# Attention and a two-layer network on one core: weight sums placed by a table, one x sum moved into the block, loads and filling laid anew, more idle matmuls

## The chip, the cores and the metric

The kernel runs on one core of a Trainium2 chip. The time is the device time of one execution in microseconds (us). Before the change it is 371.84 us, the median of three runs (371.81 to 371.89).

## What is computed

The reference, cut to what matters (q, k, v are 8 batches x 12 heads x 448 positions x 64; w_in is 768 x 2048, w_out 2048 x 768):

```python
scores = q @ k.transpose(0, 1, 3, 2) / sqrt(64) - log(448)
attn   = 1 / (1 + exp(-scores))                  # a sigmoid, no softmax
x      = (attn @ v).transpose(0, 2, 1, 3).reshape(3584, 768)
h      = x @ w_in
g      = h * (1 / (1 + exp(-beta * h)))
out    = g @ w_out
```

The kernel works in fp16 with sums in fp32.

## The kernel before

**Attention.** A *quad* g is four heads of one batch; there are 24, three to a batch. Its q and k are loaded, cast to fp16 by the DMA (`load_one`, L121), and turned by VectorE (`transpose`, L193). A *visit* (`visit`, L271) computes the scores of one quad for one tile of 128 keys, as eight matmuls that run in four row groups of the array (sixteen where the last 64 keys of two quads are taken together), and ScalarE turns them into weights with one sigmoid over four PSUM banks (`weigh_two`, L251; in the first part of the program `weigh`, L240, over two). When all keys of a quad are there, `attend` (L318) multiplies the weights with v, sixteen matmuls, and VectorE casts the result into xT (L349). v's last 64 rows are copied to the other half of the partitions first (`double_v_last`, L160).

**The dense layers** fill TensorE between visits. `early` (L729) holds the first layer of batch 0 (`dense1`, L368, L377) with ScalarE's sigmoid (L394) and VectorE's product, the gate (L395), and the second layer of tiles 0 and 1 (`plain`, L408); `second_batch` (L764) the first layer of batch 1. Some partial results of batch 0 are put aside into SBUF by VectorE (L389) and brought back into a PSUM bank by ScalarE (`bring`, L363) before they are finished. From there on the second layer goes in pairs of tiles by a scheme with seven products in place of eight (`strassen`, L633, L644), and the first layer of batches 2 and 3, 4 and 5, 6 and 7 in three *blocks* of the same scheme (`blocks`, L540, L522). The schemes need sums: of parts of w_in (S1 to S4, `in_sum`, L474), of w_out (T1, T3, T4, T6, T7, `weight_sum`, L455), of x (`x_sums`, L490) and of g (L631). VectorE makes all of them; each weight sum is cut into two parts, 18 instructions in all.

**What sets the order.** The order is written by hand (`tc.manual_schedule`); each engine runs its instructions in the order in which the program issues them. `LOADS` and `LATER` order the loads on GpSimd's queue. `BEGIN` (L858) lists the first part of the program: casts, transposes, scores, idle matmuls (`idle_units`, L840, matmuls on zeros whose result is not used), attends, dense units. Then comes a loop over 74 visits (L972). `UNITS[n]` says how many dense matmuls follow visit n, `LATE[n]` after how many of them a waiting attend is placed (99: not in this visit). `some_sum` (L908) issues one weight sum in each visit until all are made. The first x sums are issued in visits from the list `soon`, what is left of it in `first_layer` (L961) before the block starts.

**Banks.** PSUM has eight banks. In the first part of the program six belong to the scores, from `two` on four, in the blocks none; `bank` (L84) gives out the least recently used of the rest.

## Time and profile before

| What | Value |
|---|---|
| median of three runs | 371.84 us |
| profiled execution, its own time | 371.74 us |
| its span | 370.0 us |
| busy: TensorE / VectorE / ScalarE / GpSimd | 361.8 / 262.7 / 259.6 / 85.1 us |
| granted TensorE clock | 1.00 |
| software DMA queue | 22.47 MB, 40.1% of the 16 engines' span |

The span is that of the profiled execution from its first to its last instruction; 1.74 us lie around it. A row of the order of time has its start, its duration, the engine and line, the operation and in brackets the idle time before it with what ended it. TensorE's matmuls are pipelined and their ends are modelled, so starts are safer than ends. In a row of the busy time by stretch stand, after the stretch, its length and then busy time (with the count) of TensorE's matmuls, its weight loads, VectorE, ScalarE and GpSimd, then the granted clock, the DMA engines' busy share and GB/s. The chain of waits is followed back from the last instruction. Visits are numbered from 0, as the loop numbers them; visit 0 starts at 36.30 us, visit 6 at 52.69 us.

### The profile page before, as it was taken

To read this page: it belongs to the slowest core of one execution; us is meant where nothing else is said; L and a number is where in the kernel's file an instruction comes from. 1 tells how busy PE (TensorE), PEld (TensorE's weight loads), DVE (VectorE), ACT (ScalarE), POOL (GpSimd) and SP (SyncE) were. 2 spreads that over 40 slices of the span, in tenths; PEclk is the share of its full clock that TensorE was granted. 3 is DMA by queue.
4 is the path that set the end of the run, shared out by engine and by line. 5 is a ranking of instruction groups with operands and counts; after the bars stand their busy time and mean duration, and the time that the engine had idled before them with its cause. 6 is when DMAs were issued, how large, how long until landed. Compare 5 with 4: busy or idle time off the path is not lost.

```text
span 370.0 us, 6995 instructions
## 1 busy us (share of the span) xinstructions
PE 361.8 (98%) x2750; PEld 176.3 (48%) x2750; DVE 262.7 (71%) x486; ACT 259.6 (70%) x308; POOL 85.1 (23%) x125
## 2 busy tenths in 40 slices
PE   8899999999999999999999999999999999999996
PEld 5334444344444455544444455554444455556664
DVE  2636878875687876785766986779766678688664
ACT  5977967898867578877777758887777758870000
POOL 7633543311130022341131002337100002220000
PEclk9999999999999999999999999999999999999999
DMA  9999999856093110099359211004913030002332
GB/s 170 205 209 204 202 205 202 193 71 97 6 168 90 43 44 1 0 139 159 63 92 200 56 44 43 1 2 65 204 44 85 2 85 2 1 2 63 87 103 90
DMA packets 32416, 34.62 MB, mean 94 GB/s; under 512 B 9328, under 2 KB 28416, under 8 KB 32384
## 3 DMA queue, kind: packets, MB, share of 16 engines
q0 software_dynamic: 26400, 22.47, 40.1%
q1 hardware_dynamic: 5984, 11.71, 11.7%
q8 instruction: 21, 0.34, 0.4%
q14 instruction: 11, 0.09, 0.1%
HBM read 45.62 MB, written 11.01 MB: 153 GB/s over the span
## 4 chain that ended last, share of the span: by engine, by line
PE 92%; ACT 5%; DMA 1%; DVE 1%; issue 0%; SPq 0%; ACTq 0%
PE ps L644 33%; PE ps L522 26%; PE ps L229 12%; PE ps L377 10%; PE ps L335 10%; ACT attns L242 2%; ACT attns L257 2%; PE ps L408 2%; DMA gt<-in_q_dram 1%; DVE osb L663 0%; DVE xT L349 0%; DVE ps L582 0%; ACT raw L826 0%; DVE qT L200 0%; PE ps L842 0%
## 5 line engine op out<-in xcount | busy, mean ns | idle before, releaser
L257 ACT ACTIVATE attns<-ps,nlogs 128x1792 f16<-128x1792 f32 x74 | 129.9, 1755 | 42.4 <-PE ps L229 42.3
L644 PEld LDWEIGHTS <-sum 128*128 128x128 f16 x536 | 49.0, 98 | 41.7 <-issue 13.0
L536 POOL TENSOR_TENSOR gt<-attns,sg 128x448 f16<-128x448 f32 x21 | 23.9, 1139 | 146.2 <-ACT sg L533 146.2
L644 PE MATMUL ps<-w_T,sum 128*128 128x384 f16 (+2 forms) x328 | 57.5, 319 | 0.0
L229 PE MATMUL ps<-qT,kT 32*128 32x448 f16 (+3 forms) x800 | 51.9, 353 | 3.6 <-ACT attns L242 1.9
L533 ACT ACTIVATE sg<-ps,beta_sb 128x448 f32<-128x448 f32 x72 | 45.2, 632 | 8.4 <-PE ps L522 5.9
L522 PE MATMUL ps<-xT,w_S 128*128 128x448 f16 x216 | 49.2, 352 | 0.1
L522 PE MATMUL ps<-xT,w_in 128*128 128x448 f16 x216 | 49.2, 352 | 0.0
L536 DVE TENSOR_TENSOR gt<-ps,sg 128x448 f16<-128x448 f32 x72 | 44.3, 619 | 3.5 <-ACT sg L533 3.3
L663 DVE TENSOR_TENSOR osb<-ps,osb 128x384 f32<-128x384 f32 (+2 forms) x67 | 36.1, 540 | 13.1 <-PE ps L644 11.8
L349 DVE CAST xT<-ps 128x448 f16<-128x448 f32 (+1 forms) x50 | 27.9, 600 | 24.1 <-PE ps L335 24.0
L522 PEld LDWEIGHTS <-w_in 128*128 128x128 f16 x288 | 28.1, 98 | 26.4 <-issue 0.4
L335 PE MATMUL ps<-attns,v 128*64 128x448 f16 (+3 forms) x400 | 40.4, 353 | 0.0
L377 PE MATMUL ps<-xT,w_in 128*128 128x448 f16 x192 | 39.7, 353 | 0.0
L631 DVE TENSOR_TENSOR sum<-gt 128x1024 f16<-128x1024 f16 x57 | 38.4, 690 | 0.2
L644 PE MATMUL ps<-w_out,sum 128*128 128x384 f16 x208 | 37.9, 327 | 0.0
L644 PE MATMUL ps<-w_out,gt 128*128 128x384 f16 (+2 forms) x200 | 36.8, 321 | 0.0
L582 DVE TENSOR_TENSOR ps<-ps,attns 128x448 f32<-128x448 f32 x24 | 15.2, 632 | 23.4 <-PE ps L522 22.0
L522 PEld LDWEIGHTS <-w_S 128*128 128x128 f16 x216 | 21.1, 98 | 19.6 <-issue 0.3
L125 POOL DMA_DIRECT2D raw<-in_q_dram x24 | 13.4, 559 | 69.1 <-DVE kT L212 56.2
L229 PEld LDWEIGHTS <-kT 32*128 32x128 f16 (+1 forms) x800 | 13.5, 96 | 32.6 <-issue 30.2
L395 DVE TENSOR_TENSOR gt<-ps,sg 128x448 f16<-128x448 f32 x32 | 18.9, 619 | 14.1 <-ACT sg L394 13.9
(54 smaller groups left out, 346.6 us busy)
## 6 DMA issues: line engine op xcount, KB each, us to landing
out_dram<-osb SPq DMA_DIRECT2D x98, 96.0 KB, 1.9
raw<-in_q_dram POOLq DMA_DIRECT2D x23, 224.0 KB, 6.2
raw<-in_k_dram POOLq DMA_DIRECT2D x23, 224.0 KB, 6.7
v<-in_v_dram POOLq DMA_DIRECT2D x16, 192.0 KB, 8.1
w_out<-in_moe_w_out_dram POOLq DMA_DIRECT2D x4, 768.0 KB, 15.8
v<-in_v_dram POOLq DMA_DIRECT2D x16, 144.0 KB, 8.1
w_in<-in_moe_w_in_dram POOLq DMA_DIRECT2D x3, 512.0 KB, 11.1
w_in<-in_moe_w_in_dram POOLq DMA_DIRECT2D x3, 256.0 KB, 8.0
```

Source lines behind the costliest of these rows:

```text
L229: nc.tensor.matmul(sco[base : base + nk, hh, u0 : u0 + n], kT[g][lo : lo + BLK, jt * P : jt * P + nk, e], qT[g][lo : lo + BLK, c0 : c0 + n ...
L257: nc.scalar.activation(out=attns[:, slot : slot + 2].rearrange("p n h s -> p (n h) s"), in_=sco, func=AF.Sigmoid, bias=nlogs[:, 0:1], scal ...
L335: nc.tensor.matmul(av[hh * D : (hh + 1) * D, 0:n], vs[b][base : base + nk, 2 * (s % NPAIR) + hh, jt], at[base : base + nk, hh, 0:n], start ...
L349: nc.vector.tensor_copy(out=xTs[b][:, s % NPAIR, c0 : c0 + n], in_=av)
L377: nc.tensor.matmul(m1, w_in16[:, hc, dc * P : (dc + 1) * P], xTs[b][:, hc], start=fresh, stop=(hc == hi - 1), skip_group_check=lo > 0,)
L395: nc.vector.tensor_tensor(out=gt[:, dc, off : off + S], in0=m1, in1=sg, op=ALU.mult)
L522: nc.tensor.matmul(out, w[:, c, i * P : (i + 1) * P], m[:, c], start=(start and c == 0), stop=(c == KH - 1), skip_group_check=not start,)
L533: nc.scalar.activation(out=sg, in_=h, func=AF.Sigmoid, bias=0.0, scale=beta_sb[:, dc : dc + 1])
L536: return lambda: engine.tensor_tensor(out=gt[:, dc, b % 2 * S : b % 2 * S + S], in0=h, in1=sg, op=ALU.mult)
L631: nc.vector.tensor_tensor(out=sums[t, i], in0=x, in1=y, op=op)
L644: nc.tensor.matmul(m2, (x if op is None else sums[t, i])[:, dc], w[:, dc, lo:hi], start=first, stop=(dc == ND - 1), skip_group_check=i >= 4,)
L663: nc.vector.tensor_tensor(out=out, in0=in0, in1=in1, op=op)
```

## The change

- *Weight sums.* A table now says in which visit each of the 18 parts is issued, on VectorE as before. Before, one part was issued in each visit from visit 0 on, where its condition allowed it.
- *Asides.* For two of the five (3 and 4) VectorE brings the partial result back into PSUM, not ScalarE.
- *Last x sum.* The last of the x sums before a block is issued inside it, behind the first sum of D.
- *Loads.* Load 3 comes before load 4, and load 5 goes ahead of w_out's first quarter and of the second v.
- *Filling.* `UNITS` and `LATE` have new numbers, and `BEGIN` orders its last dense work and the transposes of quad 3 differently.
- *Idle matmuls.* 14 more of 256 columns, and 5 of 448 columns (`busy`), which write a bank of their own from `bank`.

The diff, cut to its core (of the tables a few lines):

```diff
+    BY_VECTOR = (3, 4)
...
-        nc.scalar.copy(out=m2s[0, dc].rearrange("p (a c) -> p a c", a=2), in_=aside(dc))
+        copy = nc.vector.tensor_copy if dc in BY_VECTOR else nc.scalar.copy
+        copy(out=m2s[0, dc].rearrange("p (a c) -> p a c", a=2), in_=aside(dc))
...
-    def blocks(b: int, other, scores: int):
+    def blocks(b: int, other, last_sum, scores: int):
...
                 nc.vector.tensor_tensor(out=D, in0=B, in1=p5, op=ALU.add)
+                while last_sum:
+                    last_sum.pop()()
...
-            ("qk", 4), ("qk", 3), ("w_in", 12, 16), ("w_out", 0, 0), ("values", 1), ("w_out", 1, 0), ("qk", 5),
+            ("qk", 3), ("qk", 4), ("w_in", 12, 16), ("qk", 5), ("w_out", 0, 0), ("values", 1), ("w_out", 1, 0),
...
+        def busy_units(n: int):
+            to = bank()
+            for _ in range(n):
+                nc.tensor.matmul(to, still[:, 0:P], still[:, 0:S], start=True, stop=True)
...
-            ("idle", 20), ("scores", 0, 0, 1), ("idle", 4), ("scores", 0, 0, 0), ("q", 0, 1), ("idle", 2), ("k", 1),
-            ("q", 1, 0), ("idle", 4), ("scores", 0, 1, 0), ("idle", 6), ("scores", 0, 1, 1), ("v", 0), ("q", 1, 1),
+            ("idle", 20), ("scores", 0, 0, 1), ("idle", 8), ("scores", 0, 0, 0), ("q", 0, 1), ("idle", 6), ("k", 1),
+            ("q", 1, 0), ("idle", 4), ("scores", 0, 1, 0), ("idle", 10), ("scores", 0, 1, 1), ("busy", 3), ("v", 0),
...
-            ("values", 1, 1), ("two",), ("visit", 2, 2), ("dense", 4), ("values", 2, 3), ("values", 2, 0),
+            ("loads",), ("values", 1, 1), ("busy", 2), ("two",), ("visit", 2, 2), ("values", 2, 3), ("dense", 4),
...
+        sums_todo = [
+            ("S3", 0, 0), ("S2", 0, 0), ("S3", 1, 1), ("S2", 1, 4), ("S4", 1, 5), ("T7", 1, 7), ("S4", 0, 9),
+            ("T1", 1, 11), ("T6", 0, 13), ("T7", 0, 13), ("T1", 0, 14), ("T3", 0, 15), ("T6", 1, 16), ("T3", 1, 16),
+            ("T4", 0, 17), ("T4", 1, 19), ("S1", 0, 29), ("S1", 1, 33),
+        ]
...
-            12, 11, 14, 9, 2, 13, 9, 10, 11, 2, 10, 0, 9, 11, 12, 11, 2, 10, 1, 10, 13, 10, 13, 2, 13, 13, 2, 11, 11,
+            11, 11, 11, 7, 2, 11, 12, 11, 12, 2, 11, 2, 11, 11, 11, 2, 11, 10, 2, 11, 10, 11, 13, 3, 12, 12, 1, 12,
...
-            while soon:
+            while len(soon) > 1:
                 soon.pop(0)()
...
-            blocks(b, fill_units, 2 if b < B - 2 else 0)
+            blocks(b, fill_units, soon, 2 if b < B - 2 else 0)
...
-            some_sum()
+            some_sums(n)
```

In the new table of sums the third number is the visit. The lines of the changed program stand a few lines lower than those of the old one (L395 is L397 there, L482 L484, L501 L503, L582 L584).

VectorE's order at visits 0 to 4, around the first weight sums (L482) and the copy of the second v's last rows (L163), before:

```order
29 L482 TENSOR_TENSOR w_S_99<-w_in_90 128x3x512
30 L395 TENSOR_TENSOR gt<-ps,sg 128x448 x2
31 L200 STREAM_TRANSPOSE qT<-raw 128x448
32 L482 TENSOR_TENSOR w_S_99<-w_in_90 128x3x512
33 L395 TENSOR_TENSOR gt<-ps,sg 128x448 x2
34 L212 STREAM_TRANSPOSE kT<-raw 128x2x4x32
35 L212 STREAM_TRANSPOSE kT<-raw 128x2x3x32
36 L482 TENSOR_TENSOR w_S_98<-w_in_90,w_S_99 128x3x512
37 L395 TENSOR_TENSOR gt<-ps,sg 128x448 x3
38 L482 TENSOR_TENSOR w_S_98<-w_in_90,w_S_99 128x3x512
39 L163 COPY v_403<-v_403 64x12x64
40 L200 STREAM_TRANSPOSE qT<-raw 128x448
```

and in the changed program (L484 the sums, L368 the two asides that VectorE brings back, L397 the gates):

```order
30 L368 COPY ps<-gt 128x448
31 L397 TENSOR_TENSOR gt<-ps,sg 128x448
32 L484 TENSOR_TENSOR w_S_99<-w_in_90 128x3x512
33 L484 TENSOR_TENSOR w_S_98<-w_in_90,w_S_99 128x3x512
34 L368 COPY ps<-gt 128x448
35 L397 TENSOR_TENSOR gt<-ps,sg 128x448 x2
36 L200 STREAM_TRANSPOSE qT<-raw 128x448
37 L484 TENSOR_TENSOR w_S_99<-w_in_90 128x3x512
38 L397 TENSOR_TENSOR gt<-ps,sg 128x448 x2
39 L212 STREAM_TRANSPOSE kT<-raw 128x2x4x32
40 L212 STREAM_TRANSPOSE kT<-raw 128x2x3x32
41 L397 TENSOR_TENSOR gt<-ps,sg 128x448 x2
42 L163 COPY v_423<-v_423 64x12x64
```

The copy of v has three sums ahead of it in place of four, the two asides stand among them, and the second part of S2 is behind it.

VectorE's order where the third block begins, before (L501 the x sums, L582 the first sum of D):

```order
310 L349 COPY xT<-ps 128x448 x2
311 L501 TENSOR_TENSOR xT<-xT 128x448
312 L501 TENSOR_TENSOR xT<-xT 128x896 x2
313 L501 TENSOR_TENSOR attns<-xT 128x1344
314 L582 TENSOR_TENSOR ps<-ps,attns 128x448
315 L536 TENSOR_TENSOR gt<-ps,sg 128x448
316 L663 TENSOR_TENSOR osb<-ps,osb 128x384
```

and in the changed program (L503 and L584):

```order
314 L349 COPY xT<-ps 128x448 x2
315 L503 TENSOR_TENSOR xT<-xT 128x448
316 L503 TENSOR_TENSOR xT<-xT 128x896 x2
317 L584 TENSOR_TENSOR ps<-ps,attns 128x448
318 L503 TENSOR_TENSOR attns<-xT 128x1344
319 L538 TENSOR_TENSOR gt<-ps,sg 128x448
320 L667 TENSOR_TENSOR osb<-ps,osb 128x384
```

The last x sum, of 1344 columns into attns, has changed places with the first sum of D.

TensorE's order after the last scores of quad 0, before:

```order
199 L229 LDWEIGHTS kT
200 L229 MATMUL ps<-qT,kT 64x224
201 L229 LDWEIGHTS kT
202 L229 MATMUL ps<-qT,kT 128x448
203 L229 LDWEIGHTS kT
```

and in the changed program (L851 the wide idle matmuls):

```order
223 L229 LDWEIGHTS kT
224 L229 MATMUL ps<-qT,kT 64x224
225 L851 LDWEIGHTS gt
226 L851 MATMUL ps<-gt 128x448
227 L851 LDWEIGHTS gt
228 L851 MATMUL ps<-gt 128x448
229 L851 LDWEIGHTS gt
230 L851 MATMUL ps<-gt 128x448
231 L229 LDWEIGHTS kT
232 L229 MATMUL ps<-qT,kT 128x448
```

Three matmuls on zeros with their weight loads stand ahead of the next visit's scores.

More of the change, by code (lines that the diff above doesn't have):

```diff
@@ L880 @@
                 idle_units(a[0])
+            elif what == "busy":
+                busy_units(a[0])
             elif what == "v":
@@ L901, with some_sums @@
         fill += list(pairs(3, 5))
-        sums_todo = [(in_sum, n, p, 0) for n in ("S3", "S2", "S4") for p in range(2)]
-        sums_todo += [(weight_sum, n, p, 0) for n in ("T7", "T6", "T1") for p in range(2)]
-        sums_todo += [(weight_sum, n, p, L1B) for n in ("T4", "T3") for p in range(2)]
-        sums_todo += [(in_sum, n, p, L1E + 4 * ND) for n in ("S1",) for p in range(2)]
-        def some_sum(n: int = 1):
-            for _ in range(n):
-                if sums_todo and at_fill[0] >= sums_todo[0][3] and (sums_todo[0][0] is in_sum or (g, jt) > (QPB + 1, 1)):
-                    f, name, part, _ = sums_todo.pop(0)
-                    f(name, part)
+        sums_todo = [
[3 rows of a table added]
+        ]
+        ready_at = {"T4": L1B, "T3": L1B, "S1": L1E}
+        behind = {"S2": ("S3",), "S4": ("S2",), "S1": ("S3",), "T4": ("T7", "T1"), "T3": ("T6",)}
+        made = set()
+        def some_sums(n: int):
+            while sums_todo and sums_todo[0][2] <= n:
+                name, part, _ = sums_todo.pop(0)
+                assert at_fill[0] >= ready_at.get(name, 0)
+                assert all((x, part) in made for x in behind.get(name, ()))
+                made.add((name, part))
+                (in_sum if name in us else weight_sum)(name, part)
         visits = [(QPB, jt, ()) for jt in range(JF + 1)]
```

10 lines of the change are left out of this document (5 added, 5 removed), and 13 rows, old and new, of tables (LATE, UNITS).

## The prediction

> **What bounds the kernel now.** I read the page's chain of waits first, then the busy time by stretch, then TensorE's order of time where TensorE has gaps.
>
> ```profile
> PE 92%; ACT 5%; DMA 1%; DVE 1%; issue 0%; SPq 0%; ACTq 0%
> ```
>
> ```profile
> 5.50:24.20 18.70, 16.10 (x200) 7.18 (x201) 9.00 (x25) 17.62 (x20) 9.54 (x15) 1.00 1.23 201
> 52.70:70.00 17.30, 16.32 (x148) 7.26 (x148) 12.58 (x21) 12.27 (x8) 3.64 (x7) 1.00 1.16 214
> 70.00:94.50 24.50, 24.44 (x209) 9.95 (x209) 15.29 (x28) 22.94 (x25) 4.87 (x9) 1.00 0.60 86
> ```
>
> The chain is TensorE's for 92%: the time is what TensorE streams plus its pauses, and an edit pays only where it removes a pause or a switch. Two stretches have pauses. From 5.5 to 24.2 us ScalarE is busy 17.62 of 18.70 us and sets the pace. From 52.7 to 70.0 TensorE lacks 1 us though no engine is full (ScalarE 12.27, VectorE 12.58 of 17.3). Its order of time there shows why; the starts are what I use, since ends are modelled:
>
> ```profile
> 52.69 0.57 PE L229 MATMUL ps<-qT,kT 32*128 32x448 f16 x8
> 53.19 1.64 PE L408 MATMUL ps<-w_out,gt 128*128 128x384 f16 x9
> 55.18 0.60 PE L229 MATMUL ps<-qT,kT 32*64 32x448 f16 x16 [0.35 <-ACT attns L257]
> ...
> 60.59 1.64 PE L335 MATMUL ps<-attns,v 64*64 64x448 f16 x16
> 62.16 0.50 PE L408 MATMUL ps<-w_out,gt 128*128 128x384 f16 x2
> 62.59 0.57 PE L229 MATMUL ps<-qT,kT 32*128 32x448 f16 x8
> ...
> 67.58 0.58 PE L229 MATMUL ps<-qT,kT 32*128 32x448 f16 x8 [0.34 <-ACT attns L257]
> 68.08 1.88 PE L377 MATMUL ps<-xT,w_in 128*128 128x448 f16 x9
> 70.06 0.57 PE L229 MATMUL ps<-qT,kT 32*128 32x448 f16 x8
> ```
>
> ```profile
> 53.37 1.75 ACT L257 ACTIVATE attns<-ps,nlogs 128x1792 f16<-128x1792 f32 x1 [1.03 <-PE ps L229]
> ```
>
> A visit (L229) fills all four score banks, ScalarE needs 1.75 us to empty them, and only then may the next visit start: 52.69 (visit), 53.37 (ScalarE starts), 55.12 (done), 55.18 (next visit). This **loop** takes 2.43 to 2.49 us. A visit itself takes 0.50 (52.69 to 53.19), or 0.53 with sixteen matmuls, so the filling between two visits must last some 1.95 us or TensorE waits. What filling lasts comes from the chain's unstalled pieces:
>
> ```profile
> 58.23 1.90 PE ps L408 x11
> ...
> 73.36 2.38 PE ps L377 x12
> ...
> 76.25 2.19 PE ps L377 x11
> ```
>
> An L377 matmul is 2.38 - 2.19 = 0.19, and every change of kind costs 0.11 (11 x 0.19 is 2.08, not 2.19); an L408 (an L644 has its shape) is then (1.90 - 0.11) / 11 = 0.163. Eleven L408 with a visit make 2.41: at the limit; twelve are free.
>
> **The change, part by part.**
>
> *The table of filling (UNITS, LATE).* Visits 6 to 11 of the old table run from 52.69 to 67.58: 14.89. Their filling is 9 L408 (1.58), 10 (1.74), 11 (1.90), attend and 2 (1.57 + 0.43), 7 and 3 (7 x 0.163 + 3 x 0.19 + 0.11 = 1.82), attend alone (1.57): 10.61, with five visits of 0.51 and one of 0.53 13.69. So 1.20 of waiting. Visit 12 has 9 L377: 68.08 to 70.06 is 1.98 against 2.19 - 2 x 0.19 = 1.81: 0.17. The new table gives visits 6 to 12 the fillings 12, 11, 12, 2 with an attend, 11 (ten and one), an attend with 2, and 11: each 1.95 or more but visit 7. These 1.37 go. Two visits at 107 have the same trouble:
>
> ```profile
> 107.43 0.58 PE L229 MATMUL ps<-qT,kT 32*128 32x448 f16 x8
> ...
> 109.92 0.60 PE L229 MATMUL ps<-qT,kT 32*64 32x448 f16 x16
> ...
> 112.45 0.58 PE L229 MATMUL ps<-qT,kT 32*128 32x448 f16 x8
> ```
>
> 2.49 and 2.53, with eleven L644 each (2.41 and 2.43): 0.18, and the new table has twelve there. In all **-1.55**. New visits of eleven L408 stand at 5 and 7: 0.02 to 0.06 each, **+0.07**. Past 200 us both tables have nine visits of about 2.41: nothing. Counted in the order of TensorE from visit 0 on, both streams hold the same matmuls, and the new one has one switch more: **+0.10**.
>
> *The sums on VectorE.* Eighteen sums before, eighteen after, 0.94 each; only their places move. One old place hurts:
>
> ```profile
> 48.23 1.80 PE ps L335 x16
> ```
>
> ```profile
> 47.69 0.65 DVE L163 COPY v<-v 64x768 f16<-64x768 f16 x1
> ```
>
> This attend takes 1.80, not 1.57: it waits for the copy of v's last rows, which stands behind a sum (S2) and ends at 48.34. The new order has three sums ahead of the copy instead of four, with S2's second part behind it: by the durations of its queue I count it done by 46.5, and the attend needs it at 47.1. **-0.23**. Later eight T sums, not three, fall between 69 and 87 us:
>
> ```profile
> L464 DVE TENSOR_TENSOR w_T<-w_out 128x1536 f16<-128x1536 f16 x6 | 5.6, 936 | 2.5 <-DMA w_out<-in_moe_w_out_dram 2.5
> ```
>
> Without its three sums VectorE has 15.29 - 2.8 = 12.5 in the 24.5 us from 70.0: 0.51 a us. From 69 to 84.6 that is 8.0, with seven sums of 0.9 14.3 of 15.6: 92% full. The gates then run 0.6 to 1.4 us behind ScalarE. Three sigmoid buffers and a free bank (1.13 us of six L377 for each dc) cover that, so I take nothing; the other end is a pause of 0.94 at each of the two places where two sums stand together (visits 13 and 16), +1.9.
>
> *Two asides brought by VectorE.*
>
> ```profile
> L366 ACT COPY ps<-gt 128x448 f32<-128x448 f32 x5 | 2.7, 537 | 0.0
> ```
>
> ScalarE loses 2 x 0.54. No row has a VectorE copy from SBUF into PSUM; by the nearest it lies between this 0.54 and the 0.65 of the copy of v, and I take 0.65. TensorE needs the second bank at the sixth matmul of visit 1 (about 40.5), and VectorE has written it by about 40.0, behind two gates and two sums. Hidden: 0; were that cover gone, at most the 0.65. ScalarE's gain is worth nothing by itself, since TensorE does not wait for it between 36 and 47.
>
> *The last x sum inside the block.*
>
> ```profile
> 299.16 0.85 DVE L501 TENSOR_TENSOR attns<-xT 128x1344 f16<-128x1344 f16 x1
> 299.73 0.81 PE L644 MATMUL ps<-w_T,sum 128*128 128x384 f16 x4
> 299.93 0.63 DVE L582 TENSOR_TENSOR ps<-ps,attns 128x448 f32<-128x448 f32 x1
> ...
> 300.61 0.73 PE L522 MATMUL ps<-xT,w_S 128*128 128x448 f16 x3
> ```
>
> In the third block four L644 from 299.73 are done at 300.38, but the next product starts at 300.61, after D's sum (L582), which stood behind the x sum. VectorE could have begun it at 299.2, or as its operand came some 0.2 later. Now it comes first and is done by about 300.0, before TensorE asks: **-0.23**. The x sum is next due in the second round, some 5 us on. In blocks one and two TensorE did not wait here: 0. The last attend before this block is also 0.10 too long (chain: 1.67), for the last weights; one L644 more in front of it covers that: **-0.10**.
>
> *Loads.*
>
> ```profile
> 29.04 0.61 POOL L154 DMA_DIRECT2D v<-in_v_dram  x1 [0.97 <-DMA raw<-in_k_dram]
> ```
>
> ```profile
> v<-in_v_dram POOLq DMA_DIRECT2D x16, 192.0 KB, 8.1
> ```
>
> The two 224 KB of load 5 go ahead of w_out and v on GpSimd's queue, so these come 448 KB / 201 GB/s = 2.2 us later. The last v was issued at 29 and takes some 8 us, so it lands near 38 and now near 40; its copy is due at 46. The last two quarters of w_out stand behind the same bytes as before, and the first T sum, which waited 2.5 us for them, waits as it did. I take 0; the other end is the 2.2.
>
> *Idle matmuls at the start.* Fourteen short and five wide ones are added.
>
> ```profile
> 6.37 17.71 ACT L242 ACTIVATE attns<-ps,nlogs 128x896 f16<-128x896 f32 x20 [1.26 <-PE ps L229]
> ```
>
> ```profile
> 6.25 0.61 PE L842 MATMUL ps<-gt 128*128 128x256 f16 x4
> ...
> 7.43 0.57 PE L229 MATMUL ps<-qT,kT 32*128 32x224 f16 x14 [0.37 <-ACT attns L242]
> 7.93 0.83 PE L842 MATMUL ps<-gt 128*128 128x256 f16 x6
> ...
> 10.81 0.69 PE L229 MATMUL ps<-qT,kT 32*128 32x224 f16 x14 [0.26 <-ACT attns L242]
> ...
> 12.62 0.57 PE L229 MATMUL ps<-qT,kT 32*128 32x448 f16 x6 [0.39 <-ACT attns L242]
> ...
> 14.88 0.38 PE L842 MATMUL ps<-gt 128*128 128x256 f16 x2 [0.20 <-DVE xT L349]
> ...
> 24.13 0.57 PE L229 MATMUL ps<-qT,kT 32*128 32x448 f16 x6 [0.53 <-ACT attns L242]
> ```
>
> A short one is (0.83 - 0.61) / 2 = 0.11, a wide one 0.19 like an L377: 14 x 0.11 + 5 x 0.19 = 2.49 of TensorE. All lie ahead of 24.13, where TensorE waits for ScalarE, which runs its twenty small activations from 6.37 to 24.08 nearly without a break. Going through them: the four at 6.7 end before the wait that ends at 7.43; those at 8.5 and 10.2 together make the scores of 10.81 late by 0.15 and so ScalarE by 0.12; the three wide ones fit into the wait before 12.6; the four at 14.88 write a bank whose cast ends 0.18 sooner, which gives back all but 0.04; the two wide ones at 23.4 end at about 23.9. **+0.04**, between 0 and 0.15.
>
> The granted clock is 1.00 in every stretch, and from 6.25 on the short ones come 0.11 apart. The Trainium skill (TensorE: Matmul & The Clock Gate, "What's actually happening") says that TensorE falls to half its clock after an idle window of about 3.4 us; by that the added matmuls keep nothing up that was down, since the longest wait of TensorE's in these rows is 0.53, and the sum would be the same.
>
> Sum: -1.55 - 0.23 - 0.23 - 0.10 + 0.07 + 0.10 + 0.04 = **-1.90**. The profiled execution took 371.74 (span 370.0); 369.84. The median is 0.10 above it: **369.9 us**.
>
> **The rivals.**
> - *VectorE's backlog from 69 to 87 us* reaches TensorE: gates late, banks and sigmoid buffers not free, ScalarE held, the visits with it. For it: 92% full. Against: 1.4 us late by my count where some 2 are allowed. One sum exposed gives 370.8, both pairs 371.8.
> - *Slower: the idle matmuls are not hidden.* If ScalarE at 6 to 24 us isn't the limit that I take it for, all 2.49 stand in the path: 369.9 + 2.45 = 372.3. It decides once more than 1.9 of the 2.49 is exposed. Against: ScalarE's 17.62 of 18.70.
> - *The tables don't do what they say*: the visits of 6 to 12 wait for something else than the score loop (keys and queries, the loads), and the 1.37 and 0.18 stay. 371.5.
> - *GpSimd beside VectorE's sums.* In the trace a carry copy took 1.28 at 46.85 beside a sum and 0.77 at 41.96.
>
> ```profile
> 41.96 0.77 POOL L443 COPY carry<-gt 128x512 f16<-128x512 f16 x1
> ...
> 46.85 1.28 POOL L443 COPY carry<-gt 128x512 f16<-128x512 f16 x1 [1.33 <-DVE gt L395]
> ```
>
> So a sum beside a copy or an issue costs GpSimd some 0.5. Four such would bring later loads 2 us late; TensorE would see that only at visit 11 or after: 369.9 to 370.4. The Trainium skill (GPSIMD Engine Reference, "8. Key points") says that GpSimd shares its SBUF interfaces with VectorE and contends with its instructions of two SBUF inputs; the trace agrees with the 1.28.
>
> **How the numbers follow.** A measurement can tell about 0.2%, 0.74 us. Forecast 369.4 to 370.4 with the GpSimd case: 0.73; somewhat better, another short wait gone: 0.06; backlog 0.11 (half of it under 371.1); tables without effect 0.05; slower 0.05. Faster by over 0.2% (under 371.1) 0.85, same 0.09, slower 0.06. Range 369.2 to 371.0.
>
> **What would show it.** Right: no step between visits 6 to 12 pays a wait for L257; the attend at 47 takes 1.57; the third block has no wait at its first D; ScalarE's last small activation ends at 24.1 as before. Wrong: TensorE waits between 69 and 87 us for VectorE or for ScalarE behind it, or the score after the second wide pair starts later than 24.3.

## The result, and the profile after

| | before | after |
|---|---|---|
| median (range) of six runs | 371.87 us (371.79 to 373.43) | 370.00 us (369.83 to 370.13) |
| profiled execution, its own time | 371.74 us | 369.92 us |
| its span | 370.0 us | 368.1 us |

The ratio is 0.9937, with an interval from 0.9918 to 0.9956, all of it under 1: faster. It is a ratio of averages, and two of the six executions before took 373.25 and 373.43, which is why it lies below that of the medians, 0.9950. The forecast was 369.9 (for the profiled execution 369.84).

The same views as before, now of the changed kernel. First the chain of waits:

```profile
PE 97%; ACT 1%; DVE 0%; issue 0%
```

TensorE's share of the chain rose from 92 to 97%, ScalarE's fell from 5 to 1. Then the busy time by stretch; the columns are those named ahead of the prediction:

```profile
5.50:24.20 18.70, 18.04 (x216) 8.62 (x216) 9.10 (x25) 17.64 (x20) 9.09 (x15) 1.00 1.22 200
...
52.70:70.00 17.30, 17.30 (x155) 7.42 (x153) 10.05 (x19) 12.67 (x10) 5.11 (x10) 1.00 1.20 219
70.00:94.50 24.50, 24.50 (x205) 10.06 (x204) 20.21 (x35) 23.07 (x23) 3.98 (x7) 1.00 0.58 84
```

From 52.7 to 70.0 TensorE is now busy for the whole stretch, with 155 matmuls where 148 stood. From 5.5 to 24.2 it is busy 1.94 us more, with idle matmuls, and ScalarE's 17.64 is what it was (17.62). From 70 to 94.5 VectorE went from 15.29 to 20.21: the T sums came here. TensorE's order of time where the pauses were:

```profile
51.77 2.12 PE L410 MATMUL ps<-w_out,gt 128*128 128x384 f16 x12
53.83 0.60 PE L229 MATMUL ps<-qT,kT 32*64 32x448 f16 x16
54.36 1.96 PE L410 MATMUL ps<-w_out,gt 128*128 128x384 f16 x11
56.30 0.58 PE L229 MATMUL ps<-qT,kT 32*128 32x448 f16 x8
...
64.37 1.64 PE L335 MATMUL ps<-attns,v 64*64 64x448 f16 x16
65.94 0.55 PE L379 MATMUL ps<-xT,w_in 128*128 128x448 f16 x2
66.43 0.57 PE L229 MATMUL ps<-qT,kT 32*128 32x448 f16 x8
66.94 2.26 PE L379 MATMUL ps<-xT,w_in 128*128 128x448 f16 x11
```

None of these rows ends in a bracket: no visit waits for L257 long enough to be marked. The eleven L410 from 54.36 last 0.04 longer than the 1.90 that they cost; that is one of the two new short visits. Twelve L410 last from 51.77 to 53.83, 2.06, as long as twelve cost (0.11 + 12 x 0.163). The attend at visit 4 and VectorE around it:

```profile
46.83 0.50 PE L410 MATMUL ps<-w_out,gt 128*128 128x384 f16 x2
47.26 1.64 PE L335 MATMUL ps<-attns,v 64*64 64x448 f16 x16
48.83 0.57 PE L229 MATMUL ps<-qT,kT 32*128 32x448 f16 x8
```

```profile
45.92 0.35 DVE L163 COPY v<-v 64x768 f16<-64x768 f16 x1
...
47.79 1.01 DVE L484 TENSOR_TENSOR w_S<-w_in,w_S 128x1536 f16<-128x1536 f16 x1
```

The copy of v is done at 46.27, the attend starts at 47.26 and takes 1.57 to the next visit, where it took 1.80. The second part of S2 stands behind. The third block:

```profile
297.81 0.63 DVE L584 TENSOR_TENSOR ps<-ps,attns 128x448 f32<-128x448 f32 x1 [0.19 <-PE ps L524]
...
298.11 0.81 PE L648 MATMUL ps<-w_T,sum 128*128 128x384 f16 x4
...
298.35 0.85 DVE L503 TENSOR_TENSOR attns<-xT 128x1344 f16<-128x1344 f16 x1
...
298.76 0.73 PE L524 MATMUL ps<-xT,w_S 128*128 128x448 f16 x3
```

D's sum runs ahead of the x sum; four L648 take 0.65 from 298.11, and the next product starts at 298.76 without a wait.

**Where the time came from.** I added up what TensorE waits from visit 0 to the end of the last block: the start of each group of matmuls to the start of the next, less what these matmuls and the change of kind cost where nothing waits. The sum is 2.54 us before and 0.50 after, and the 0.50 has no piece over 0.12. One change of kind more takes back 0.10. The stretch up to visit 0 is 0.10 longer (36.30 to 36.40): the first small activation starts at 6.50, not 6.37. So -2.04 + 0.10 + 0.10 = -1.84; the spans differ by 1.9.

### The profile page after: what moved, and what is told of

Its sections match the earlier page's. It is cut to its first block, busy times and chain, and to the rows that moved or that the text cites. A ratio compares the mean times of both kernels' runs of the same rounds, so it can differ in the third digit from the quotient of the medians.

```text
span 368.1 us, 7034 instructions
## 1 busy us (share of the span) xinstructions
PE 363.1 (99%) x2769; PEld 176.8 (48%) x2769; DVE 263.8 (72%) x488; ACT 258.7 (70%) x306; POOL 83.4 (23%) x125
## 4 chain that ended last, share of the span: by engine, by line
PE 97%; ACT 1%; DVE 0%; issue 0%
PE ps L648 34%; PE ps L524 26%; PE ps L229 12%; PE ps L379 10%; PE ps L335 10%; PE ps L410 3%; PE ps L846 2%; ACT attns L242 1%; DVE osb L667 0%; DVE xT L349 0%; PE ps L851 0%; DVE gt L840 0%
## 5 line engine op out<-in xcount | busy, mean ns | idle before, releaser
L257 ACT ACTIVATE attns<-ps,nlogs 128x1792 f16<-128x1792 f32 x74 | 129.8, 1755 | 41.2 <-PE ps L229 41.1
L648 PEld LDWEIGHTS <-sum 128*128 128x128 f16 x536 | 48.9, 98 | 42.1 <-issue 13.6
L648 PE MATMUL ps<-w_T,sum 128*128 128x384 f16 (+2 forms) x328 | 58.2, 319 | 0.0
L229 PE MATMUL ps<-qT,kT 32*128 32x448 f16 (+3 forms) x800 | 51.2, 354 | 0.1
L538 DVE TENSOR_TENSOR gt<-ps,sg 128x448 f16<-128x448 f32 x72 | 44.3, 619 | 2.4 <-ACT sg L535 2.2
L667 DVE TENSOR_TENSOR osb<-ps,osb 128x384 f32<-128x384 f32 (+2 forms) x67 | 36.1, 541 | 13.7 <-PE ps L648 12.0
L349 DVE CAST xT<-ps 128x448 f16<-128x448 f32 (+1 forms) x50 | 27.9, 600 | 23.0 <-PE ps L335 23.0
L524 PEld LDWEIGHTS <-w_in 128*128 128x128 f16 x288 | 28.1, 98 | 26.4 <-issue 0.4
L379 PE MATMUL ps<-xT,w_in 128*128 128x448 f16 x192 | 40.1, 353 | 0.0
L648 PE MATMUL ps<-w_out,sum 128*128 128x384 f16 x208 | 37.9, 327 | 0.0
L648 PE MATMUL ps<-w_out,gt 128*128 128x384 f16 (+2 forms) x200 | 36.6, 320 | 0.0
L584 DVE TENSOR_TENSOR ps<-ps,attns 128x448 f32<-128x448 f32 x24 | 15.2, 633 | 24.3 <-PE ps L524 24.3
L335 PEld LDWEIGHTS <-v 128*64 128x64 f16 (+1 forms) x400 | 17.6, 108 | 20.8 <-issue 13.3
L379 PEld LDWEIGHTS <-w_in 128*128 128x128 f16 x192 | 17.2, 98 | 21.3 <-issue 7.6
## 6 DMA issues: line engine op xcount, KB each, us to landing
w_in<-in_moe_w_in_dram POOLq DMA_DIRECT2D x3, 512.0 KB, 11.1
```

The lines of the kernel that those rows point to most:

```text
L229: nc.tensor.matmul(sco[base : base + nk, hh, u0 : u0 + n], kT[g][lo : lo + BLK, jt * P : jt * P + nk, e], qT[g][lo : lo + BLK, c0 : c0 + n ...
L257: nc.scalar.activation(out=attns[:, slot : slot + 2].rearrange("p n h s -> p (n h) s"), in_=sco, func=AF.Sigmoid, bias=nlogs[:, 0:1], scal ...
L335: nc.tensor.matmul(av[hh * D : (hh + 1) * D, 0:n], vs[b][base : base + nk, 2 * (s % NPAIR) + hh, jt], at[base : base + nk, hh, 0:n], start ...
L349: nc.vector.tensor_copy(out=xTs[b][:, s % NPAIR, c0 : c0 + n], in_=av)
L379: nc.tensor.matmul(m1, w_in16[:, hc, dc * P : (dc + 1) * P], xTs[b][:, hc], start=fresh, stop=(hc == hi - 1), skip_group_check=lo > 0,)
L524: nc.tensor.matmul(out, w[:, c, i * P : (i + 1) * P], m[:, c], start=(start and c == 0), stop=(c == KH - 1), skip_group_check=not start,)
```

## The experiments

My theory was the sum on record: the tables of filling give most, by ending waits for the score loop; the order of sums and the x sum give the rest; asides, loads and idle matmuls give nothing. The rivals: VectorE's backlog takes a part back, the idle matmuls stand in the path, the tables act on something else. Each kernel runs beside runs of the kernel before, with medians from 371.94 to 372.30, and the ratio is to these. "Waits" is the sum just described, of the profiled execution; it begins with visit 0 and holds nothing of what lies ahead. It is the sharper measure: the start of the first activation moves by up to 0.6 us from profile to profile (6.31 to 6.89), and all that comes later moves with it.

| Kernel | median, range (runs) | ratio to before, interval | waits |
|---|---|---|---|
| before | 371.87 (6) | 1 | 2.54 |
| after | 370.00, 369.83 to 370.13 (6) | 0.9937, 0.9918 to 0.9956 | 0.50 |
| e1: before + new UNITS, LATE | 371.23, 370.92 to 372.24 (11) | 0.9972, 0.9959 to 0.9985 | 1.60 |
| e2: after with old UNITS, LATE | 371.69, 371.52 to 372.16 (12) | 0.9974, 0.9961 to 0.9988 | 2.28 |
| e3: after, old idle matmuls | 369.96, 369.88 to 371.32 (6) | 0.9939, 0.9919 to 0.9960 | 0.49 |
| e12: the kernel of e3 again | 370.22, 369.90 to 371.39 (10) | 0.9950, 0.9933 to 0.9967 | as e3 |
| e4: before + x sum in the block | 371.76, 371.56 to 373.68 (12) | 0.9984, 0.9969 to 1.0000 | 2.31 |
| e6: after, one sum per visit | 370.86, 370.41 to 371.49 (12) | 0.9959, 0.9946 to 0.9973 | 0.97 |
| e7: after, T1, T6, T7 made twice | 373.02, 372.90 to 375.53 (12) | 1.0023, 1.0007 to 1.0038 | 3.51 |
| e9: after, asides by ScalarE | 370.45, 370.19 to 370.92 (6) | 0.9950, 0.9931 to 0.9969 | 0.81 |
| e8: after, old order of loads | 370.32, 369.99 to 370.48 (6) | 0.9943, 0.9925 to 0.9961 | 0.50 |
| e5: after, added idle matmuls twice | 371.75, 371.45 to 372.15 (12) | 0.9987, 0.9976 to 0.9999 | 0.51 |
| e10: after, first 20 idle matmuls only | 371.94, 371.65 to 372.44 (12) | 0.9990, 0.9978 to 1.0001 | 0.50 |
| e11: before + the added idle matmuls | 372.08, 371.82 to 372.34 (12) | 0.9992, 0.9978 to 1.0006 | 2.52 |

**e1, the tables alone.** The two new lists stand in the kernel before; nothing else is changed.

```diff
-            12, 11, 14, 9, 2, 13, 9, 10, 11, 2, 10, 0, 9, 11, 12, 11, 2, 10, 1, 10, 13, 10, 13, 2, 13, 13, 2, 11, 11,
+            11, 11, 11, 7, 2, 11, 12, 11, 12, 2, 11, 2, 11, 11, 11, 2, 11, 10, 2, 11, 10, 11, 13, 3, 12, 12, 1, 12,
...
-            0: 8, 1: 1, 2: 4, 3: 99, 4: 2, 5: 99, 6: 6, 7: 99, 8: 99, 10: 99, 12: 5, 13: 2, 14: 1, 15: 99, 16: 2,
+            0: 2, 1: 2, 2: 4, 3: 99, 4: 2, 5: 9, 6: 6, 7: 99, 8: 99, 9: 2, 10: 99, 12: 2, 13: 2, 14: 1, 16: 1, 19: 6,
```

> The kernel before with the new UNITS and LATE alone. Theory (the score loop of 2.43 to 2.49 us bounds short visits): the waits of visits 6 to 12 and 27, 28 go (-1.55) and the 0.10 of the last attend, +0.17 for short visits 5 and 7 and the one switch: 371.84 - 1.5 = 370.3, between 370.1 and 370.6, and visits 6 to 12 show no wait for L257. Rival (VectorE's order of sums was the bound, the tables only follow it): under 0.5 of gain, 371.4 or more, and the same visits still wait.

Measured 371.23, not 370.3. The waits of visits 6 to 12 and of the old place at 107 are gone, as they should be. But new ones came: 0.21 at visit 1, 0.18 at visit 4, 0.47 at visit 27, and the block's 0.23 stayed; that is 1.09, and 1.60 - 0.50 = 1.10. The largest, in this kernel's order of time:

```profile
106.97 1.64 PE L644 MATMUL ps<-w_T,sum 128*128 128x384 f16 x9
...
107.46 0.95 DVE L482 TENSOR_TENSOR w_in<-w_in 128x1536 f16<-128x1536 f16 x1
108.32 1.21 DVE L663 TENSOR_TENSOR osb<-ps,osb 128x384 f32<-128x384 f32 x2
108.93 0.65 PE L644 MATMUL ps<-w_T,sum 128*128 128x384 f16 x3 [0.32 <-DVE osb L663]
```

The second part of S1 (L482, 107.46) stands on VectorE ahead of the two L663 that empty a bank; the tenth L644 needs that bank and starts at 108.93. Nine matmuls at 0.163 from 106.97 would have let it start at 108.44. After the change the same visit shows no sum, and an L667 at 106.88:

```profile
106.39 2.12 PE L648 MATMUL ps<-w_T,sum 128*128 128x384 f16 x12
...
106.88 0.55 DVE L667 TENSOR_TENSOR osb<-ps,osb 128x384 f32<-128x384 f32 x1
108.06 0.56 DVE L667 TENSOR_TENSOR osb<-ps,osb 128x384 f32<-128x384 f32 x1 [0.64 <-PE ps L648]
```

So the tables' 1.55 is not the tables' alone: without the moved sums and asides about 0.9 of it comes back elsewhere. In my sum the tables had 1.55 and the placing of sums 0.23; the total was right and the shares were not.

**e2, the reverse: after with the old lists.** The diff is that of e1, turned round.

> The changed kernel with the old UNITS and LATE. Theory: the visits 6 to 12 and 27, 28 wait again, some 1.4 us of the 1.9: 370.0 + 1.4 = 371.4 (371.2 to 371.6). Rival (the order of sums, the asides and the loads carry the gain): 370.5 or less.

Measured 371.69, a little above the upper end. TensorE's order shows the old waits where they were:

```profile
53.09 1.64 PE L410 MATMUL ps<-w_out,gt 128*128 128x384 f16 x9
55.08 0.60 PE L229 MATMUL ps<-qT,kT 32*64 32x448 f16 x16 [0.35 <-ACT attns L257]
...
65.48 1.64 PE L335 MATMUL ps<-attns,v 64*64 64x448 f16 x16
67.47 0.58 PE L229 MATMUL ps<-qT,kT 32*128 32x448 f16 x8 [0.34 <-ACT attns L257]
```

Visits 6 to 12 wait 0.41, 0.20, 0.17, 0.41 and 0.17, 1.36 in all; 0.20 comes at visits 27 and 28 and 0.10 at the last attend, as reckoned. Not reckoned is 0.22 at visit 17, where the gate that frees TensorE's next bank starts at 82.01 behind two T sums (80.19 and 81.14). This settles what the waits of visits 6 to 12 are: the score loop, with too little filling; it disposes of the rival that the tables act on something else.

**e4, the x sum alone,** put into the kernel before.

```diff
                 nc.vector.tensor_tensor(out=D, in0=B, in1=p5, op=ALU.add)
+                while last_sum:
+                    last_sum.pop()()
...
-            while soon:
+            while len(soon) > 1:
                 soon.pop(0)()
```

> The kernel before with the last x sum inside the block alone. Theory: the wait of 0.23 at the first D of the third block goes and nothing else: 371.84 - 0.23 = 371.6. Rival (the x sum is then late for the second round or for the gates behind it): a wait in the second round of a block, 371.84 or more.

The waits fall from 2.54 to 2.31, the 0.23 of the block; every other one stands. The time, 371.76, is in line, though 0.23 us by itself is at the edge of what the interval tells (0.9969 to 1.0000). The trace decides here.

**e6, one sum in each visit again,** with the rest of the change.

```diff
-            some_sums(n)
+            some_sum()
```

> The changed kernel with the old order of weight sums, one in each visit from visit 0. Theory (with the new filling the old places of the sums make TensorE wait): the 0.47 at visit 27 comes, behind the second part of S1, and 0.1 to 0.6 at visits 1 to 4, where VectorE has four sums and two asides ahead of the copy of v: 370.0 + 0.8 = 370.8, between 370.5 and 371.1. Rival (the tables alone carry the gain, and VectorE's order is free): 370.1 or less.

Measured 370.86, and 0.48 more of waiting: all at visit 27, the place that e1 showed. With the new lists and VectorE's two asides the old order of sums costs nothing at visits 1 to 4. The copy of v, which I had put at -0.23 for the new order, ends at 47.45 here, ahead of the attend at 47.59; in e2, with the new order and the old lists, it ends at 47.04 ahead of 48.28. In e1, with the new lists alone, it ends at 47.77, just behind the attend's start at 47.75, and 0.08 of waiting is left. So either part ends that wait, the lists alone not quite. What I had overlooked is the copy's own length. Before, in e4 and in e11 it took 0.65, where it began while a carry copy of GpSimd was still running (46.85 to 48.13 before); in every other kernel here it took 0.35 or 0.36, and with that it would have ended at 48.04, ahead of the attend at 48.16. Whether the carry copy drew it out is not shown: in e2 a carry copy starts 0.03 behind it, and the copy of v takes its 0.35. What the table of sums gives for certain is S1, moved from visits 26 and 27 to 29 and 33.

**e7, the T sums doubled.** T1, T6 and T7 are made twice with the same values, six instructions more on VectorE.

```diff
-                (in_sum if name in us else weight_sum)(name, part)
+                for _ in range(2 if name in ("T6", "T7", "T1") else 1):
+                    (in_sum if name in us else weight_sum)(name, part)
```

> The changed kernel with the six parts of T1, T6 and T7 each made twice, 5.6 us more for VectorE between 54 and 81 us. Theory (VectorE is some 92% full from 69 to 85 us and 0.6 to 1.4 us late, with cover for about 2): two to three more sums in a row at visits 13 and 14 use the cover up, and TensorE waits 0.5 to 2 us there: 371.0. Rival (the cover is wider than counted): 370.2 or less.

Measured 373.02, 3.0 more than after, 2.0 more than I expected, and slower than before (1.0007 to 1.0038). The backlog that I had weighed as a rival is real; it needs a good deal more of sums, though. In this kernel's order VectorE runs sums back to back:

```profile
71.41 3.81 DVE L466 TENSOR_TENSOR w_T<-w_out 128x1536 f16<-128x1536 f16 x4
75.14 1.15 DVE L397 TENSOR_TENSOR gt<-ps,sg 128x448 f16<-128x448 f32 x2
76.20 1.94 DVE L466 TENSOR_TENSOR w_T<-w_out 128x1536 f16<-128x1536 f16 x2
```

and TensorE waits behind it, at visit 12 for a cast (L349), later for gates (L397):

```profile
75.89 2.08 PE L335 MATMUL ps<-attns,v 64*64 64x448 f16 x16
78.73 0.54 PE L379 MATMUL ps<-xT,w_in 128*128 128x448 f16 x2 [0.76 <-DVE gt L397]
...
85.69 0.38 PE L335 MATMUL ps<-attns,v 64*64 64x448 f16 x2 [0.71 <-DVE gt L397]
```

In these brackets stands the idle time behind a modelled end; from start to start the waits are 0.45 at visit 12, 1.28 at visit 15, and 0.78 and 0.52 at visit 18: 3.03, of 5.6 us of sums (6 x 0.94) put in. VectorE is busy for 22.66 of the 24.50 us from 70, against 20.21 in the changed kernel. So the cover is there, but it has an end: 4.9 us more than before (15.29 to 20.21) cost nothing, and six more sums cost 3.0.

**e9, all asides by ScalarE.**

```diff
-    BY_VECTOR = (3, 4)
+    BY_VECTOR = ()
```

> The changed kernel with all five asides brought back by ScalarE. By the prediction nothing: 370.0. By what the run with the tables alone showed, TensorE waits some 0.2 us in the dense matmuls of visit 1 for the aside that ScalarE brings behind a visit's sigmoid, now that visit 0 has eleven matmuls and not twelve: 370.2. Rival (ScalarE's 1.08 us come back in full): 371.0.

Measured 370.45. The waits show 0.31 more, 0.21 at visit 1 and 0.10 at visit 4. I had taken zero, since TensorE did not wait for ScalarE between 36 and 47 before. ScalarE's order in this kernel:

```profile
38.89 0.54 ACT L368 COPY ps<-gt 128x448 f32<-128x448 f32 x1
39.35 1.16 ACT L396 ACTIVATE sg<-ps,beta_sb 128x448 f32<-128x448 f32 x2
40.39 1.76 ACT L257 ACTIVATE attns<-ps,nlogs 128x1792 f16<-128x1792 f32 x1
```

and TensorE's:

```profile
39.31 0.57 PE L229 MATMUL ps<-qT,kT 32*128 32x448 f16 x8
39.81 2.26 PE L379 MATMUL ps<-xT,w_in 128*128 128x448 f16 x11
42.21 0.58 PE L229 MATMUL ps<-qT,kT 32*128 32x448 f16 x8
```

The visit's scores are done at about 39.8, but ScalarE empties the banks only from 40.39, as the aside and two sigmoids come first; it is done at 42.15, and the next visit starts at 42.21. With VectorE's copy the same activation starts at 39.73 after a visit at 39.10. The new lists took one L377 out of visit 0 and so bring visit 1 closer to ScalarE; the aside on VectorE pays for that.

**e8, the old order of loads.**

```diff
-            ("qk", 3), ("qk", 4), ("w_in", 12, 16), ("qk", 5), ("w_out", 0, 0), ("values", 1), ("w_out", 1, 0),
+            ("qk", 4), ("qk", 3), ("w_in", 12, 16), ("w_out", 0, 0), ("values", 1), ("w_out", 1, 0), ("qk", 5),
```

> The changed kernel with the old order of the later loads (load 4 before 3, load 5 behind the second v and half of w_out). Theory: no transfer is late in either order, 370.0 within 0.2, and TensorE's waits after visit 0 are those of the changed kernel, some 0.5 us. Rival (the new filling needs load 5 or load 3 early): a wait of VectorE's transposes for raw and a wait of TensorE behind it, 370.4 or more.

Measured 370.32, 0.3 more than after. From visit 0 on the waits are 0.50 as after, and no place differs; but visit 0 starts at 36.85, not 36.40, though the first activation (6.53) and the last of the twenty (done at 24.22) are where they were after the change (6.50 and 24.19). VectorE's and TensorE's rows between show the cause:

```profile
30.33 0.41 DVE L200 STREAM_TRANSPOSE qT<-raw 128x224 f32<-128x224 f32 x1 [2.01 <-DMA raw<-in_q_dram]
30.67 1.65 DVE L397 TENSOR_TENSOR gt<-ps,sg 128x448 f16<-128x448 f32 x3
...
31.84 5.08 PE L379 MATMUL ps<-xT,w_in 128*128 128x448 f16 x26 [0.26 <-DVE gt L397]
```

The transpose of quad 3 waits 2.01 for its load, the gates behind it run late, and TensorE waits for a gate. The 48 L379 ahead of visit 0 last 9.60 from start to start; after the change, where the transpose starts at 28.21 and the first gate at 29.61, they last 9.18. So this is the rival of the expectation, with 0.42 us. Before, with the same order of loads, the transposes of quad 3 came only at 33.82 and waited for nothing. The new `BEGIN` has them early, and load 3 ahead of load 4 pays for that.

**e3, the added idle matmuls taken out,** from `BEGIN`.

```diff
-            ("q", 1, 0), ("idle", 4), ("scores", 0, 1, 0), ("idle", 10), ("scores", 0, 1, 1), ("busy", 3), ("v", 0),
+            ("q", 1, 0), ("idle", 4), ("scores", 0, 1, 0), ("idle", 6), ("scores", 0, 1, 1), ("v", 0),
```

> The changed kernel without the 14 short and 5 wide idle matmuls that it added. Theory (ScalarE's twenty activations hide them): 370.0, within 0.1, and TensorE's score after the second pair of wide ones starts as before at about 24.1. Rival one (they stand in the path): up to 2.4 less, 367.6. Rival two (they keep TensorE's clock up): matmuls twice as far apart somewhere before 24 us, and more than 370.3.

The span is the same, 368.1. In this kernel's busy time by stretch TensorE has 16.03 where the changed kernel has 18.04, and ScalarE has 17.61 where it has 17.64:

```profile
5.50:24.20 18.70, 16.03 (x196) 7.19 (x196) 9.11 (x25) 17.61 (x20) 8.93 (x15) 1.00 1.23 202
```

Two us of matmuls are hidden wholly: visit 0 starts at 36.40 in both. One of the six executions, 371.32, had a granted clock of 0.995 (another, 371.13, a whole one). That made me ask whether the idle matmuls do have an effect, in some executions only; e5, e10, e11 and e12 go after it.

**e5, the added idle matmuls twice.**

```diff
-            ("q", 1, 0), ("idle", 4), ("scores", 0, 1, 0), ("idle", 10), ("scores", 0, 1, 1), ("busy", 3), ("v", 0),
+            ("q", 1, 0), ("idle", 4), ("scores", 0, 1, 0), ("idle", 14), ("scores", 0, 1, 1), ("busy", 6), ("v", 0),
```

> The changed kernel with the added idle matmuls doubled: 14 short and 5 wide ones more. Theory (the first 24 us have room for one such set and hardly for two): the three places with 0.44 more before 12 us delay ScalarE by some 0.3 to 0.4 each, the rest fits: 370.0 + 1.0 = 371.0, between 370.7 and 371.4. Rival (room for all): 370.2 or less.

Measured 371.75, more than the 371.0 that I gave: 1.55 of the 2.49 us stand in the path. ScalarE's order shows it. One group of twenty without a break before and after the change is now in pieces:

```profile
6.31 1.53 ACT L242 ACTIVATE attns<-ps,nlogs 128x896 f16<-128x896 f32 x2 [1.25 <-PE ps L229]
8.22 1.91 ACT L242 ACTIVATE attns<-ps,nlogs 128x896 f16<-128x896 f32 x2 [0.38 <-PE ps L229]
```

The brackets say that ScalarE waits for scores (L229), which stand behind idle matmuls; four more such pauses follow by 18.3 us. One set fits into TensorE's pauses, and a second doesn't.

**e10, no idle matmuls after the first twenty.** This takes out the eighteen of the kernel before as well.

```diff
-            ("idle", 20), ("scores", 0, 0, 1), ("idle", 8), ("scores", 0, 0, 0), ("q", 0, 1), ("idle", 6), ("k", 1),
-            ("q", 1, 0), ("idle", 4), ("scores", 0, 1, 0), ("idle", 10), ("scores", 0, 1, 1), ("busy", 3), ("v", 0),
+            ("idle", 20), ("scores", 0, 0, 1), ("scores", 0, 0, 0), ("q", 0, 1), ("k", 1),
+            ("q", 1, 0), ("scores", 0, 1, 0), ("scores", 0, 1, 1), ("v", 0),
```

> The changed kernel without any idle matmul after the first twenty, old ones too. Theory: TensorE waits for ScalarE in their place, ScalarE's twenty activations still take 17.7 us, and the time is 370.0 within 0.2. Rival (they keep TensorE's clock up): matmuls of twice the spacing between 6 and 24 us, ScalarE's stretch longer, 370.5 or more.

Here my theory fell. Less work on TensorE, and 371.94: 1.94 slower than after. The busy time by stretch of this kernel, where the column behind GpSimd's is the granted clock:

```profile
5.50:9.00 3.50, 2.24 (x35) 0.93 (x35) 0.54 (x3) 2.14 (x3) 1.86 (x4) 1.00 1.13 172
9.00:11.00 2.00, 0.94 (x16) 0.42 (x16) 0.98 (x3) 2.00 (x3) 1.25 (x2) 0.79 1.50 185
11.00:13.00 2.00, 1.56 (x16) 0.42 (x16) 1.46 (x6) 1.72 (x3) 1.64 (x4) 0.50 1.30 209
...
14.30:16.75 2.45, 2.45 (x28) 1.16 (x26) 0.76 (x3) 1.65 (x2) 1.12 (x3) 0.50 1.23 209
16.75:20.00 3.25, 3.21 (x44) 1.62 (x44) 2.83 (x8) 3.15 (x4) 1.00 (x2) 0.96 1.15 207
```

TensorE was busy for 2.24 + 0.94 of the 5.5 us up to 11.0 (58%; before 2.99 + 1.73 in the same stretch, 86%), and from about 10.2 to 17.0 its clock is half (0.79 over the 2.00 us from 9 is 0.84 us at half, 0.96 over the 3.25 from 16.75 is 0.26). Its order of time ahead of that and in it:

```profile
5.67 1.30 PE L229 MATMUL ps<-qT,kT 32*128 32x224 f16 x18
7.86 0.80 PE L229 MATMUL ps<-qT,kT 32*128 32x224 f16 x16 [0.90 <-ACT attns L242]
9.45 0.57 PE L229 MATMUL ps<-qT,kT 32*128 32x224 f16 x14 [0.79 <-ACT attns L242]
...
11.24 1.56 PE L229 MATMUL ps<-qT,kT 32*128 32x224 f16 x16 [0.53 <-ACT attns L242]
```

Sixteen scores that take 0.80 at 7.86 take 1.56 at 11.24. No pause ahead of the drop is longer than 0.90. The slow scores starve ScalarE, and visit 0 starts at 38.16, 1.75 later than after the change. All twelve executions of this kernel have a mean clock of 0.985 to 0.991.

**e11, the added idle matmuls alone,** in the kernel before, with e12 beside it.

```diff
-            ("q", 1, 0), ("idle", 4), ("scores", 0, 1, 0), ("idle", 6), ("scores", 0, 1, 1), ("v", 0), ("q", 1, 1),
+            ("q", 1, 0), ("idle", 4), ("scores", 0, 1, 0), ("idle", 10), ("scores", 0, 1, 1), ("busy", 3), ("v", 0), ("q", 1, 1),
```

> The kernel before with the added idle matmuls alone (14 short, 5 wide). Theory (they do nothing where the clock is whole, but keep it whole in every execution; of the kernel before's executions about three in ten had a mean granted clock of 0.995 and 373.4 us): the lowest times are those of the kernel before, 371.8 to 372.0, and none or one of some twelve executions has a clock of 0.995. Rival (the lower clock has nothing to do with idle matmuls): two to five of twelve at 0.995.

> The same kernel as the changed one without its added idle matmuls, once more, to count: theory: one to five of the executions at a clock of 0.995 and some 1.4 us more (371.3), the others at 369.9. Rival: none at 0.995.

The median, 372.08, is no better than that of before with a whole clock: nothing is gained in such an execution, and the waits are those of before (2.52). What changes is how often the clock is not whole. Executions with a mean granted clock of 0.995 or less, over all kernels but e10 (of before, the runs beside the experiments):

| idle matmuls | kernels | executions | of them at 0.995 or less |
|---|---|---|---|
| as before | before | 94 | 25 |
| as before | e1, e3, e4, e12 | 39 | 5 |
| with the added ones | after, e2, e5, e6, e7, e8, e9, e11 | 78 | 1 |

Of e11's own twelve none, and of the twenty executions of before beside them four: that alone would decide nothing. The 30 of 133 against 1 of 78 are far apart, and beside the runs of before on the chip of e5, e6, e7 and e9 it was 7 of 29 against 1 of 42. These counts mix in the rest of the change, though. Where the idle matmuls alone differ, they are small: 0 of 12 (e11) against 25 of 94, and 0 of 6 (after) against 2 of 16 (e3, e12). All point the same way. In e12, as expected, one of ten has 0.995 (371.19); but 370.84 and 371.39 came with a whole clock, as did six of before's from 372.73 to 374.33. What makes those longer is not known. An execution of before at 0.995 takes 373.41 in the median, the others 371.95: 1.46 more. Only e10 has a profile of an execution with the drop; that in before's 0.995 the clock drops in the same stretch and from the same cause is argued, not seen.

## Why the prediction was right, and where it was not

The time was right for mostly the right reasons. By its steps:

| Step | Predicted | Measured | Shown by |
|---|---|---|---|
| filling: waits of visits 6 to 12, 27, 28 | -1.55 | 1.56 gone (1.37 + 0.19) | before against after; e2 brings them back |
| new visits of eleven L408 | +0.07 | +0.07 (0.04 and 0.03) | after |
| one change of kind more | +0.10 | +0.10, what remains of the sum | not tried by itself |
| copy of v in time | -0.23 | -0.23; with the new lists alone 0.08 would be left | e2, e6, e1 |
| x sum in the block, last attend | -0.33 | -0.23 and -0.10 | e4 for the first; e2 has the second back |
| asides by VectorE | 0 | -0.3 against after without them | e9 |
| loads | 0 | -0.4 against after without the new order | e8 |
| VectorE from 69 to 87 | 0 | 0; of 5.6 more, 2.6 would still be covered | after, e7 |
| idle matmuls in the path | +0.04 | 0.00 | e3 |
| idle matmuls "keep nothing up" | 0 | 1.46 in about one execution of four, in part argued | clock counts, e10 |

*What held.* The score loop and its price of filling: visit by visit the waits worked out from the order of before (1.20 and 0.17) are those that e2 brings back, and the new table ends them. VectorE's backlog stayed below what the sigmoid buffers and banks cover: the gates at 72.74 and 80.79 run 0.6 and 0.8 us behind their sigmoids (done at 72.1 and 80.0).

*The parts do not add up as I set them down.* The step on asides failed: "ScalarE's gain is worth nothing by itself, since TensorE does not wait for it between 36 and 47". That was read from the kernel before, in which twelve L377 stood at visit 0. With eleven there, ScalarE's aside comes ahead of the score activation and holds the next visit. Likewise the table of sums was costed at the copy of v alone; its larger part is S1 at visit 27 (0.48), a wait that before doesn't have, and which the new lists would have made. And the step on loads asked only whether v and w_out come late, and took 0; with the transposes of quad 3 moved ahead, load 3 would have come 0.4 too late in the old order. All three were costs that one part of the change makes and another takes away. A sum against the whole change couldn't go wrong by them, since cost and cure cancel and neither was in it; on this point the time came right by luck and not by the reckoning. The expectation for e1 did go wrong, by 0.9 us.

*The idle matmuls.* The step was "by that the added matmuls keep nothing up that was down, since the longest wait of TensorE's in these rows is 0.53". The profile of before at 1.00 is one execution, and three runs between 371.81 and 371.89 had hidden that others are at 0.995. And e10 shows a drop without a pause of more than 0.90. So the longest pause is not the measure. The busy share of a stretch of some microseconds fits: from 5.5 to 11.0 it is 58% where the clock fell, 86% where it held at least in the profiled execution, 100% after the change. It can be put closer, as the clock records of the traces show it to change only every 3.41 us (below). In e10 TensorE was busy for 1.58 of the 3.41 us ahead of the drop (46%), then for 2.07 (61%) and the clock stayed at half, then for all 3.41, and the clock was whole again. In the profile of before it held through a window with 2.55 of 3.42 (75%, from 22.17, five windows behind its first record). Where the limit lies between 46 and 75%, and whether the share alone decides, these runs don't tell. The median of the prediction wasn't touched by it, as it was set against an execution with a whole clock; an average of before is some 0.4 us (25 of 94 times 1.46) above its median, and this share goes too.

*The rivals.* "Slower, the idle matmuls are not hidden" is excluded by e3, and e5 shows from which point it would have held. "The tables don't do what they say" is excluded by e2. GpSimd beside VectorE's sums: a carry copy takes 0.61 to 0.62 with no sum beside it, and up to 1.34 beside one (before, at 44.19). The 0.77 that I took for a free one ran 0.30 beside a sum. The price "or an issue" was wrong: before, the issues of loads and of v beside a sum take 0.53 to 0.65, and 0.53 to 0.62 without one. After the change all four carry copies take 0.61 to 0.62, and no wait of TensorE's follows from them.

## What to carry to other kernels

Where an engine with a fixed loop (here ScalarE, 2.43 to 2.49 us a visit) alternates with another's filling, count each visit's filling against the loop and move units from the full visits to the short ones; then look in each visit again for what was hidden by the old surplus, since the copies, sums and loads of the other engines were placed for the old one. Test such a change whole and part by part: the table of filling alone was worth 0.6 to 0.7 us of the 1.9, since its own new waits are taken away only by the other parts. And read the granted clock of many executions, not of the one profiled: work that no profile of an undisturbed execution misses can still keep the clock up.

## What the runs showed of the hardware that I had not expected

- **The clock changes in whole windows.** The clock records of e10's trace have it whole from 6.75 to 10.17 us, half to 16.99 and whole again: 3.41 and 6.83 us, once and twice the same. Before's is whole from 5.11 to 370.33, the changed kernel's from 5.92 to 367.74: 107 and 106 times 3.413. Ahead of its first record the clock was half too: in e3, whose record begins at 3.87, the first twenty idle matmuls come 0.21 apart up to there and 0.11 behind it. In the fourteen profiles the record begins anywhere from 3.87 to 7.04, and the four latest have the four latest first activations (6.70 to 6.89). A mean clock of 0.995 over 371.6 us is 2 x 0.005 x 371.6 = 3.7 us of half clock (3.3 to 4.1 by its rounding); the twelve of e10 stand at 0.991 (6.7) and at 0.985 or 0.986 (10.4 to 11.1). The Trainium skill (TensorE: Matmul & The Clock Gate, "What's actually happening") tells of an activity window of about 3.4 us that runs freely, whatever the kernel does; one, two and three such windows would be 3.4, 6.8 and 10.2, which agrees but for the two executions at 0.985, somewhat above. That it runs freely would also be why the same program drops in one execution and not in the next. But the rule of that page of the Trainium skill ("Why this matters for your kernels") against idle gaps of over 3 us does not cover e10, with none over 0.90.
- **A drop is cheaper than it looks.** Half a clock over 6.8 us would cost 3.4 us of streaming; e10's span is 1.8 longer than after's. TensorE had pauses there, and part of what ran slowly ran in them.
- **A copy by VectorE from SBUF into a PSUM bank** takes 0.62, against 0.54 for ScalarE's; I had taken 0.65. From the groups of instructions of the changed kernel, with the mean in ns behind the comma:

```profile
L368 DVE COPY ps<-gt 128x448 f32<-128x448 f32 x2 | 1.2, 620 | 0.0
```

It is slower than ScalarE's and was still the better one, as ScalarE was the engine that held the next visit.
